# Retention and a gated MLP on one core: moving loads, masks and conversions of the first pairs

## The chip, the cores and the metric

One core of one Trainium2 chip. The time is device microseconds of one execution, over several executions; the traces' span (first to last instruction) is 1.7 to 1.9 us shorter. An execution that is more than 1.5 % above its kernel's fastest is marked slow and left out of ratios. "Pair" is the unit of the first half of the kernel: 128 time steps of two batch rows, all eight heads; there are twelve, and two pairs make a group of 512 tokens for the MLP.

## The reference

A retention layer (linear attention with a decay per head), then an MLP whose gate is h·cos(h):

```python
B, H, S, D = q.shape                       # 4, 8, 768, 64
gamma = 1.0 - 2.0 ** (-5.0 - np.arange(H))
for t in range(S):
    state = gamma * state + k_t^T v_t      # per batch row and head, 64 x 64
    y[:, :, t] = scale * q_t @ state
x = y as (B*S, H*D)                        # 3072 x 512
h = x @ w_in                               # w_in 512 x 2048
out = (h * np.cos(h)) @ w_out              # w_out 2048 x 512, out in fp32
```

Inputs are fp32 in HBM; the kernel works in bf16.

## The kernel before

A pair p passes these stages. q and v are scaled by powers of gamma (`conv_q`, `conv_v`), k is cast (`conv_k`); q and k are transposed by TensorE (`stage_t`) or, from the fifth pair on, by DMA (`stage_t_dma`); `stage_a` makes the scores and `stage_m` masks them on VectorE; `stage_y` makes the output ("Y", copied by ScalarE into `xt`) and updates the state. The MLP's first half is "F" (`unit_f`, or `pair_f` for one pair's 256 tokens; ScalarE makes the cosine, VectorE the product), its second half "O" (`unit_o`). Buffers, with cuts:

```python
PRE = 5                                    # fp32 buffers of q, k, v, two batch rows each
def load(eng, p, names):                   # nc.sync: hardware queue; nc.gpsimd: software queue
    ...
    eng.dma_start(out=t[p % PRE][b], in_=src[...])
def conv_q(p, eng):
    for b in range(2):
        eng.tensor_tensor(out=qs[p % NB][:, b], in0=qf[p % PRE][b], in1=bc(gq, p % NC), op=ALU.mult)
def stage_m(p, item):                      # two masks for one batch row
    ...
        nc.vector.tensor_tensor(out=am[p % 2][b][j], in0=ap[j], in1=mask..., op=ALU.mult)
        banks.give(bk[j])
```

The order in which instructions are written is the order on each engine. The parts that the change touches:

```python
    ...
    load(nc.gpsimd, 3, ("k0", "q0", "k1", "q1", "v0", "v1"))
    load(nc.sync, 4, ("q0", "q1"))                     # fifth pair, at the very start
    load(nc.gpsimd, 4, ("k0", "k1", "v0", "v1"))
    ...
    stage_t(1, True)                                   # one copy on ScalarE, one on VectorE
    attend(1)                                          # scores and masks
    pair_f(0, 0)
    stage_y(1, nc.scalar.copy)
    pair_f(1, 0)
    ...
    for part in range(3):
        for j in range(4):
            unit_o(0, j, part)
            if part == 2 and j == 0:
                stage_t(2, None)
    for b in range(2):
        stage_m(2, stage_a(2, b))                      # third pair: scores, masks
    conv_v(2, nc.vector)                               # then v
    conv_q(3, nc.gpsimd)
    load(nc.sync, 5, ("q0", "q1", "v0"))
    load(nc.gpsimd, 5, ("k0", "k1", "v1"))
    conv_v(3, nc.gpsimd)
    for j in range(4):
        unit_o(0, j, 3)
        if j == 2:
            stage_y(2, nc.scalar.copy)
    ...
    attend(4)
    o_units(1, 0, 4)
    later(4)                                           # Y of the fifth pair, loads of the eighth
    attend(5)
    ahead(6)                                           # seventh pair: conversions
    stage_t_dma(6)
```

Of the kernel before, what the change touches and what calls it, by code (L numbers as in the profile page):

```python
# [30 lines left out]
def kernel(  # L31
# [9 lines left out]
    nc = tc.nc  # L41
# [10 lines left out]
    PRE = 5  # L52
# [11 lines left out]
    def sb(shape, dt, name):  # L64
        return const.tile(shape, dt, name=name)
# [15 lines left out]
    qf = [[sb([128, H, D], FP32, f"qf{i}_{b}") for b in range(2)] for i in range(PRE)]  # L81
    kf = [[sb([128, H, D], FP32, f"kf{i}_{b}") for b in range(2)] for i in range(PRE)]
    vf = [[sb([128, H, D], FP32, f"vf{i}_{b}") for b in range(2)] for i in range(PRE)]
    ob = [sb([128, DM], FP32, f"ob{i}") for i in range(4)]
    NB = 3
    qs = [sb([128, 2, H, D], BF16, f"qs{i}") for i in range(NB)]
    ks = [sb([128, 2, H, D], BF16, f"ks{i}") for i in range(NB)]
    vs = [sb([128, 2, H, D], BF16, f"vs{i}") for i in range(NB)]
# [13 lines left out]

    SRC = {"q": (qf, q), "k": (kf, k), "v": (vf, v)}

    def load(eng, p, names):
        bp, c = divmod(p, NC)
        for n in names:
            t, src = SRC[n[0]]
            b = int(n[1])
            eng.dma_start(  # L110
                out=t[p % PRE][b],
                in_=src[2 * bp + b, :, ds(c * C, C)].rearrange("h t d -> t h d"))

    def load_w_in(r):
# [36 lines left out]
    def bc(g, c):  # L151
        return g[:, c, :].unsqueeze(2).to_broadcast([128, H, D])

    def conv_q(p, eng):
        for b in range(2):
            eng.tensor_tensor(out=qs[p % NB][:, b], in0=qf[p % PRE][b],  # L156
                              in1=bc(gq, p % NC), op=ALU.mult)

    def conv_v(p, eng):
        for b in range(2):  # L160
            eng.tensor_tensor(out=vs[p % NB][:, b], in0=vf[p % PRE][b],  # L161
                              in1=bc(gk, p % NC), op=ALU.mult)

    def conv_k(p, on_act):
        for b in range(2):
            if on_act:
                nc.scalar.copy(out=ks[p % NB][:, b], in_=kf[p % PRE][b])  # L167
            else:
                nc.vector.tensor_copy(out=ks[p % NB][:, b], in_=kf[p % PRE][b])

    def stage_t(p, split, fill=0):
        n = p % NB
        for b in range(2):
            if fill:
                warm(fill * b)
            bank = banks.take()
            tr = bank.bitcast(BF16).rearrange("p (w a t) -> p w a t", w=2, a=HP)
            for w, src in enumerate((qs[n], ks[n])):
                for a in range(HP):
                    nc.tensor.transpose(tr[:, w, a, :], src[:, b, 2 * a : 2 * a + 2, :], ident)  # L180
            if split is None or split and b == 1:
                nc.vector.tensor_copy(out=qkt[n][:, :, b], in_=tr)
            else:
                nc.scalar.copy(out=qkt[n][:, :, b], in_=tr)  # L184
            banks.give(bank)

    def stage_t_dma(p):
        n = p % NB
        for w, src in enumerate((qs[n], ks[n])):
            nc.sync.dma_start_transpose(  # L190
                out=qkt[n][:, w].rearrange("p b a t -> p (b a) t"),
                in_=src.rearrange("p b h d -> p (b h d)"))

    def qt(n, b, a):
        return qkt[n][:, 0, b, a, :]

    def kt(n, b, a):
        return qkt[n][:, 1, b, a, :]

    def stage_a(p, b):  # L200
        n = p % NB
        bk = [banks.take(), banks.take()]
        ap = [t.rearrange("p (a t) -> p a t", a=HP) for t in bk]
        for a in range(HP):
            for j in range(2):
                po = 64 * j
                nc.tensor.matmul(ap[j][:, a, :], lhsT=kt(n, b, a)[po : po + 64, :],  # L207
                                 rhs=qt(n, b, a)[po : po + 64, :],
                                 tile_position=(po, 0))
        return b, bk, ap  # L210

    def stage_m(p, item):
        b, bk, ap = item
        for j in range(2):
            nc.vector.tensor_tensor(  # L215
                out=am[p % 2][b][j], in0=ap[j],
                in1=mask.unsqueeze(1).to_broadcast([128, HP, 128]), op=ALU.mult)
            banks.give(bk[j])

    def stage_y(p, copy_st=nc.vector.tensor_copy):  # L220
        c = p % NC
        n = p % NB
        for b in range(2):
            bank = banks.take()
            yp = bank.rearrange("p (a t) -> p a t", a=HP)
            for a in range(HP):
                if c > 0:
                    for j in range(2):
                        nc.tensor.matmul(  # L229
                            yp[ts(j, 64), a, :], lhsT=stb[p % 2][:, b, a, ts(j, 64)],  # L230
                            rhs=qt(n, b, a), start=True, stop=False,
                            skip_group_check=True)
                for j in range(2):
                    nc.tensor.matmul(  # L234
                        yp[ts(j, 64), a, :], lhsT=vs[n][:, b, 2 * a + j, :],
                        rhs=am[p % 2][b][j][:, a, :], start=(c == 0), stop=True,
                        skip_group_check=True)
            nc.scalar.copy(out=xt[(p // 2) % 2][:, :, ts(2 * (p % 2) + b, C)], in_=yp)  # L238
            banks.give(bank)
        if c == NC - 1:  # L240
            return
        for b in range(2):
            for a in range(HP):
                for j in range(2):
                    h = 2 * a + j
                    nc.tensor.matmul(  # L246
                        st_ps[ts(j, 64), b, a, :], lhsT=ks[n][:, b, h, :],
                        rhs=vs[n][:, b, h, :], start=(c == 0 and b == 0 and a == 0),
                        stop=True, skip_group_check=True)
        for j in range(2):  # L250
            copy_st(out=stb[(p + 1) % 2][ts(j, 64), :, :, ts(j, 64)], in_=st_ps[ts(j, 64)])  # L251
# [21 lines left out]
    def pair_f(p, r, parts=(0, 1)):  # L273

        g, hf = divmod(p, 2)
        for f in [4 * r + 2 * i for i in parts]:
            bank = banks.take()
            for e in range(2):
                for i in range(KIN):
                    nc.tensor.matmul(bank[:, ts(e, 256)], lhsT=w_in_t(i, f + e),  # L280
                                     rhs=xt[g % 2][:, i, ts(hf, 256)],
                                     start=(i == 0 and e == 0), stop=(i == KIN - 1),
                                     skip_group_check=True)
            act(bank, gt[g % 2][:, f : f + 2, ts(hf, 256)])
            banks.give(bank)
# [33 lines left out]
    def attend(p):  # L319
        for it in [stage_a(p, b) for b in range(2)]:  # L320
            stage_m(p, it)
# [8 lines left out]
    load_w_out(3)  # L330
    load(nc.gpsimd, 2, ("v0", "v1"))
    load(nc.gpsimd, 3, ("k0", "q0", "k1", "q1", "v0", "v1"))
    load(nc.sync, 4, ("q0", "q1"))
    load(nc.gpsimd, 4, ("k0", "k1", "v0", "v1"))

    warm(10)
    conv_q(0, nc.vector)
# [7 lines left out]
    warm(6)  # L345
    stage_y(0, nc.scalar.copy)
    warm(2)
    stage_t(1, True)
    attend(1)
    pair_f(0, 0)  # L350
    banks.give(spare)
    stage_y(1, nc.scalar.copy)
    pair_f(1, 0)
    for f in range(4, 16):
        unit_f(0, f)
# [3 lines left out]
    for part in range(3):  # L359
        for j in range(4):  # L360
            unit_o(0, j, part)
            if part == 2 and j == 0:
                stage_t(2, None)
    for b in range(2):
        stage_m(2, stage_a(2, b))
    conv_v(2, nc.vector)
    conv_q(3, nc.gpsimd)
    load(nc.sync, 5, ("q0", "q1", "v0"))
    load(nc.gpsimd, 5, ("k0", "k1", "v1"))
    conv_v(3, nc.gpsimd)  # L370
    for j in range(4):
        unit_o(0, j, 3)
        if j == 2:
            stage_y(2, nc.scalar.copy)
    conv_q(4, nc.gpsimd)
    conv_v(4, nc.gpsimd)
    conv_k(3, True)
    pair_f(2, 0)
    stage_t(3, None)
    pair_f(2, 1)  # L380
    attend(3)
    conv_k(4, True)
    stage_t_dma(4)
    load(nc.sync, 6, ("q0", "q1", "v0"))
    load(nc.gpsimd, 6, ("k0", "k1", "v1"))
    pair_f(2, 2)
    pair_f(2, 3)
    stage_y(3, nc.scalar.copy)
    conv_q(5, nc.gpsimd)
    conv_v(5, nc.gpsimd)  # L390
    pair_f(3, 0)
    conv_k(5, True)
    stage_t_dma(5)
    for r in range(1, 4):
        pair_f(3, r)

    def ahead(p):
        if p < NP:
            conv_q(p, nc.gpsimd)
            conv_k(p, True)  # L400
            conv_v(p, nc.gpsimd)
# [7 lines left out]
    def o_units(g, a, b):  # L409
        for u in range(a, b):  # L410
            unit_o(g, *divmod(u, 4))

    attend(4)
    o_units(1, 0, 4)
    later(4)
    attend(5)
    ahead(6)
    stage_t_dma(6)
    o_units(1, 4, 8)
    later(5)  # L420

    for g in range(2, NG + 1):
        for s in range(16):
            hf, r = divmod(s, 8)
            p = 2 * (g + 1) + hf
# [48 lines left out]
```

## Time and profile before

| | before |
|---|---|
| time, median of 3 executions | 219.04 us (218.5 to 220.6) |
| span of the profiled execution | 217.6 us |
| TensorE / VectorE / ScalarE / GpSimd busy | 94 / 54 / 53 / 39 % |

The page has busy shares, a row per engine of 40 slices in tenths, and TensorE's granted clock in tenths. The chain of waits goes back from the last instruction to what released each step: start, duration in us, engine, tile and line. Of the views behind the prediction one is not shown there, the chain of the kernel before around the seventh pair's scores (L207), from 74 to 104 us:

```profile
79.09 3.47 PE bank L294 x16
82.57 4.65 DMA qkt<-ks
87.21 0.05 issue
87.26 0.62 PE bank L207 x16
```

TensorE's next scores follow a transposing DMA that is issued at 82.57 and lands at 87.21.

### The profile page before, as it was taken

To read this page: it belongs to the slowest core of one execution; us is meant where nothing else is said; L and a number is where in the kernel's file an instruction comes from. 1 tells how busy PE (TensorE), PEld (TensorE's weight loads), DVE (VectorE), ACT (ScalarE), POOL (GpSimd) and SP (SyncE) were. 2 spreads that over 40 slices of the span, in tenths; PEclk is the share of its full clock that TensorE was granted. 3 is DMA by queue.
4 is the path that set the end of the run, shared out by engine and by line. 5 is a ranking of instruction groups with operands and counts; after the bars stand their busy time and mean duration, and the time that the engine had idled before them with its cause. 6 is when DMAs were issued, how large, how long until landed. Compare 5 with 4: busy or idle time off the path is not lost.

```text
span 217.6 us, 4150 instructions
## 1 busy us (share of the span) xinstructions
PE 203.5 (94%) x1637; PEld 114.0 (52%) x1637; DVE 117.2 (54%) x186; ACT 115.0 (53%) x184; POOL 84.9 (39%) x98
## 2 busy tenths in 40 slices
PE   7587999985998998999999999999999999999992
PEld 2357654533898754555554544644545444444440
DVE  4377673465494962786876556656565244333000
ACT  5656873125689545476665565554535644454120
POOL 7975323899996909476951600000000000000000
PEclk9799999998899999999999999999999999999998
DMA  6999999999599889999994551051011001110221
GB/s 150 329 258 196 201 213 289 291 343 344 160 187 275 163 221 197 228 214 259 222 312 102 131 148 48 0 149 48 0 51 48 18 31 51 48 48 2 96 76 71
DMA packets 55844, 33.83 MB, mean 155 GB/s; under 512 B 47248, under 2 KB 49552, under 8 KB 55824
## 3 DMA queue, kind: packets, MB, share of 16 engines
q1 hardware_dynamic: 49472, 17.70, 35.6%
q0 software_dynamic: 6208, 15.73, 27.1%
q8 instruction: 13, 0.21, 0.4%
q10 hardware_dynamic: 144, 0.13, 0.2%
q14 instruction: 7, 0.06, 0.1%
HBM read 27.26 MB, written 6.29 MB: 154 GB/s over the span
## 4 chain that ended last, share of the span: by engine, by line
PE 83%; DVE 6%; DMA 5%; ACT 3%; issue 1%; SPq 0%; DVEq 0%; ACTq 0%
PE bank L294 37%; PE bank L268 30%; PE bank L280 7%; DVE am L215 3%; PE bank L207 3%; DMA qf<-in_q_dram 3%; DMA qkt<-ks 2%; DVE vs L161 2%; PE bank L234 2%; PE bank L229 2%; PE bank L180 1%; PE st_ps L246 1%; ACT xt L238 1%; ACT cosb L259 1%; PE bank L316 1%
## 5 line engine op out<-in xcount | busy, mean ns | idle before, releaser
L263 DVE TENSOR_TENSOR gt<-bank,cosb 128x512 bf16<-128x512 f32 x96 | 65.7, 690 | 63.9 <-ACT cosb L259 63.4
L259 ACT ACTIVATE cosb<-bank,halfpi 128x512 bf16<-128x512 f32 x96 | 65.8, 688 | 54.0 <-PE bank L268 47.5
L294 PE MATMUL bank<-w_out_sb,gt 128*128 128x512 bf16 x384 | 93.9, 382 | 0.0
L268 PE MATMUL bank<-xt,w_in 128*128 128x512 bf16 x304 | 75.0, 380 | 0.0
L294 PEld LDWEIGHTS <-gt 128*128 128x128 bf16 x384 | 36.9, 98 | 43.3 <-issue 0.6
L268 PEld LDWEIGHTS <-w_in 128*128 128x128 bf16 x304 | 33.8, 114 | 30.7
L215 DVE TENSOR_TENSOR am<-bank,mask 128x512 bf16<-128x512 f32 x48 | 30.2, 682 | 4.0 <-PE bank L207 4.0
L306 ACT COPY ob<-bank 128x512 f32<-128x512 f32 x23 | 13.5, 587 | 26.5 <-PE bank L294 26.4
L156 POOL TENSOR_TENSOR qs<-qf,gq 128x512 bf16<-128x512 f32 x18 | 18.6, 1045 | 19.5 <-DMA qf<-in_q_dram 19.3
L161 POOL TENSOR_TENSOR vs<-vf,gk 128x512 bf16<-128x512 f32 x20 | 21.2, 1078 | 5.0 <-DMA vf<-in_v_dram 3.3
L110 POOL DMA_DIRECT2D kf<-in_k_dram x23 | 20.8, 907 | 5.8 <-DMA w_in<-in_moe_w_in_dram 2.8
L280 PE MATMUL bank<-xt,w_in 128*128 128x256 bf16 x160 | 19.0, 277 | 1.3 <-ACT xt L238 1.3
L280 PEld LDWEIGHTS <-w_in 128*128 128x128 bf16 x160 | 17.5, 115 | 2.3 <-issue 1.7
L167 ACT CAST ks<-kf 128x512 bf16<-128x512 f32 x24 | 13.9, 617 | 6.6 <-DMA kf<-in_k_dram 6.5
L110 POOL DMA_DIRECT2D vf<-in_v_dram x16 | 14.2, 889 | 5.0 <-DMA w_out_sb<-in_moe_w_out_dram 4.9
L238 ACT CAST xt<-bank 128x512 bf16<-128x512 f32 x24 | 12.9, 588 | 5.5 <-DVE gt L263 3.0
L234 PE MATMUL bank<-am,vs 128*64 128x128 bf16 x192 | 11.8, 221 | 2.6 <-DVE vs L161 2.2
L234 PEld LDWEIGHTS <-vs 128*64 128x64 bf16 x192 | 10.0, 110 | 3.8 <-DVE vs L161 2.5
L207 PE MATMUL bank<-qkt 64*128 64x128 bf16 x192 | 8.1, 225 | 3.0 <-ACT qkt L184 1.3
L229 PEld LDWEIGHTS <-stb 128*64 128x64 bf16 x160 | 8.7, 109 | 3.8 <-issue 3.3
L229 PE MATMUL bank<-qkt,stb 128*64 128x128 bf16 x160 | 10.6, 223 | 0.0
L251 DVE CAST stb<-st_ps 64x512 bf16<-64x512 f32 x12 | 8.2, 687 | 3.9 <-PE st_ps L246 3.7
(38 smaller groups left out, 73.6 us busy)
## 6 DMA issues: line engine op xcount, KB each, us to landing
kf<-in_k_dram POOLq DMA_DIRECT2D x23, 256.0 KB, 5.9
out_dram<-ob SPq DMA_DIRECT2D x23, 256.0 KB, 2.1
qf<-in_q_dram SPq DMA_DIRECT2D x19, 256.0 KB, 5.0
vf<-in_v_dram POOLq DMA_DIRECT2D x16, 256.0 KB, 6.1
vf<-in_v_dram SPq DMA_DIRECT2D x8, 256.0 KB, 6.5
w_in<-in_moe_w_in_dram POOLq DMA_DIRECT2D x4, 512.0 KB, 13.4
w_out_sb<-in_moe_w_out_dram POOLq DMA_DIRECT2D x4, 512.0 KB, 16.4
qf<-in_q_dram POOLq DMA_DIRECT2D x5, 256.0 KB, 7.6
```

What stands on the lines that cost most here:

```text
L110: eng.dma_start(out=t[p % PRE][b], in_=src[2 * bp + b, :, ds(c * C, C)].rearrange("h t d -> t h d"))
L156: eng.tensor_tensor(out=qs[p % NB][:, b], in0=qf[p % PRE][b], in1=bc(gq, p % NC), op=ALU.mult)
L161: eng.tensor_tensor(out=vs[p % NB][:, b], in0=vf[p % PRE][b], in1=bc(gk, p % NC), op=ALU.mult)
L215: nc.vector.tensor_tensor(out=am[p % 2][b][j], in0=ap[j], in1=mask.unsqueeze(1).to_broadcast([128, HP, 128]), op=ALU.mult)
L229: nc.tensor.matmul(yp[ts(j, 64), a, :], lhsT=stb[p % 2][:, b, a, ts(j, 64)], rhs=qt(n, b, a), start=True, stop=False, skip_group_check=True)
L234: nc.tensor.matmul(yp[ts(j, 64), a, :], lhsT=vs[n][:, b, 2 * a + j, :], rhs=am[p % 2][b][j][:, a, :], start=(c == 0), stop=True, skip_grou ...
L238: nc.scalar.copy(out=xt[(p // 2) % 2][:, :, ts(2 * (p % 2) + b, C)], in_=yp)
L259: nc.scalar.activation(out=cb, in_=bank, func=AF.Sin, bias=halfpi)
L263: nc.vector.tensor_tensor(out=out, in0=bank, in1=cb, op=ALU.mult)
L268: nc.tensor.matmul(bank, lhsT=w_in_t(i, f), rhs=xt[g % 2][:, i, :], start=(i == 0), stop=(i == KIN - 1))
L280: nc.tensor.matmul(bank[:, ts(e, 256)], lhsT=w_in_t(i, f + e), rhs=xt[g % 2][:, i, ts(hf, 256)], start=(i == 0 and e == 0), stop=(i == KIN ...
L294: nc.tensor.matmul(bank, lhsT=gt[g % 2][:, f, ts(j, 128)], rhs=w_out_sb[:, f, :], start=(f == 0), stop=(f == KOUT - 1))
```

## The change

Its intent: keep the hardware DMA queue empty while the weights load (the fifth pair is loaded into the third's buffers, so its loads cannot start before those are read); spread the third pair's scores and masks between O units, with v scaled ahead of the masks; move half an F pair behind the second and the fourth pair's Y; convert and transpose the seventh pair earlier. Cut to its core:

```diff
+    SLOT = [0, 1, 2, 3, 2, 4, 0, 1, 3, 2, 4, 0]        # buffer of each pair, in place of p % PRE
...
-    load(nc.sync, 4, ("q0", "q1"))
-    load(nc.gpsimd, 4, ("k0", "k1", "v0", "v1"))
...
-    stage_t(1, True)
+    stage_t(1, None)                                   # both copies on VectorE
     attend(1)
-    pair_f(0, 0)
+    pair_f(0, 0, (0,))
     stage_y(1, nc.scalar.copy)
+    pair_f(0, 0, (1,))
...
             if part == 2 and j == 0:
                 stage_t(2, None)
-    for b in range(2):
-        stage_m(2, stage_a(2, b))
-    conv_v(2, nc.vector)
+                conv_v(2, nc.vector)
+            elif part == 2 and j == 1:
+                stage_m(2, stage_a(2, 0))
+            elif part == 2 and j == 3:
+                stage_m(2, stage_a(2, 1))
+    conv_k(3, True)
     conv_q(3, nc.gpsimd)
+    load(nc.sync, 4, ("q0", "q1"))
+    load(nc.gpsimd, 4, ("k0", "k1", "v0", "v1"))
+    conv_v(3, nc.gpsimd)
     load(nc.sync, 5, ("q0", "q1", "v0"))
     load(nc.gpsimd, 5, ("k0", "k1", "v1"))
-    conv_v(3, nc.gpsimd)
...
-        if j == 2:
+        if j == 1:
             stage_y(2, nc.scalar.copy)
...
-    pair_f(2, 3)
+    pair_f(2, 3, (0,))
     stage_y(3, nc.scalar.copy)
+    pair_f(2, 3, (1,))
...
+    conv_q(6, nc.gpsimd)                               # ahead of the sixth pair's last F pair
+    conv_k(6, True)
+    conv_v(6, nc.gpsimd)
     pair_f(3, 3)
...
     attend(4)
+    stage_t_dma(6)
     o_units(1, 0, 4)
     later(4)
     attend(5)
-    ahead(6)
-    stage_t_dma(6)
```

Left out of this cut: the old place of `conv_k(3, True)`, and `conv_q(4)` and `conv_v(4)`, which are now written behind `attend(3)`.

More of the change, by code (lines that the diff above doesn't have):

```diff
@@ L110, in load @@
             eng.dma_start(
-                out=t[p % PRE][b],
+                out=t[SLOT[p]][b],
                 in_=src[2 * bp + b, :, ds(c * C, C)].rearrange("h t d -> t h d"))
@@ L155, in conv_q @@
         for b in range(2):
-            eng.tensor_tensor(out=qs[p % NB][:, b], in0=qf[p % PRE][b],
+            eng.tensor_tensor(out=qs[p % NB][:, b], in0=qf[SLOT[p]][b],
                               in1=bc(gq, p % NC), op=ALU.mult)
@@ L160, in conv_v @@
         for b in range(2):
-            eng.tensor_tensor(out=vs[p % NB][:, b], in0=vf[p % PRE][b],
+            eng.tensor_tensor(out=vs[p % NB][:, b], in0=vf[SLOT[p]][b],
                               in1=bc(gk, p % NC), op=ALU.mult)
@@ L166, in conv_k @@
             if on_act:
-                nc.scalar.copy(out=ks[p % NB][:, b], in_=kf[p % PRE][b])
+                nc.scalar.copy(out=ks[p % NB][:, b], in_=kf[SLOT[p]][b])
             else:
-                nc.vector.tensor_copy(out=ks[p % NB][:, b], in_=kf[p % PRE][b])
+                nc.vector.tensor_copy(out=ks[p % NB][:, b], in_=kf[SLOT[p]][b])
     def stage_t(p, split, fill=0):
@@ L363 @@
                 stage_t(2, None)
-    for b in range(2):
-        stage_m(2, stage_a(2, b))
-    conv_v(2, nc.vector)
+                conv_v(2, nc.vector)
[4 more added lines that the diff above has]
+    conv_k(3, True)
     conv_q(3, nc.gpsimd)
+    load(nc.sync, 4, ("q0", "q1"))
+    load(nc.gpsimd, 4, ("k0", "k1", "v0", "v1"))
+    conv_v(3, nc.gpsimd)
     load(nc.sync, 5, ("q0", "q1", "v0"))
     load(nc.gpsimd, 5, ("k0", "k1", "v1"))
-    conv_v(3, nc.gpsimd)
     for j in range(4):
         unit_o(0, j, 3)
-        if j == 2:
+        if j == 1:
             stage_y(2, nc.scalar.copy)
-    conv_q(4, nc.gpsimd)
-    conv_v(4, nc.gpsimd)
-    conv_k(3, True)
     pair_f(2, 0)
@@ L381 @@
     attend(3)
+    conv_q(4, nc.gpsimd)
+    conv_v(4, nc.gpsimd)
     conv_k(4, True)
@@ L393 @@
     stage_t_dma(5)
-    for r in range(1, 4):
-        pair_f(3, r)
+    pair_f(3, 1)
+    pair_f(3, 2)
+    conv_q(6, nc.gpsimd)
+    conv_k(6, True)
+    conv_v(6, nc.gpsimd)
+    pair_f(3, 3)
     def ahead(p):
```

## The prediction

> **What bounds the kernel now.** I read the page first (busy shares, then the slices), then the chain of waits in order of time, TensorE's waits, the timeline where TensorE stopped, and the time to landing of single loads. The page first: row PE is TensorE's busy share of each fortieth of the span (5.44 us), PEclk its granted clock, both in tenths.
>
> ```profile
> PE 203.5 (94%) x1637; PEld 114.0 (52%) x1637; DVE 117.2 (54%) x186; ACT 115.0 (53%) x184; POOL 84.9 (39%) x98
> PE   7587999985998998999999999999999999999992
> PEclk9799999998899999999999999999999999999998
> DMA  6999999999599889999994551051011001110221
> ```
>
> TensorE bounds the kernel; every other engine is near half. Counting slices from 0, there is no hole from slice 16 (87 us) to the last. All that can be won lies before: slices 0 to 3 (to 22 us), slice 9 (49 to 54 us, busy 5, clock 8) with slice 10's clock of 8, and slices 12 and 15. The change touches no matmul: it can only fill holes, and the full stretch after 87 us then starts that much sooner.
>
> The chain of what ended last, 44 to 70 us (start, duration, what):
>
> ```profile
> 44.81 0.37 PE bank L207 x8
> ...
> 45.78 0.55 DVE am L215
> ...
> 46.38 1.28 DVE am L215 x2
> 47.66 4.30 DVE vs L161 x2
> ...
> 53.12 1.82 PE bank L294 x4
> 54.94 2.20 PE bank L280 x16
> ...
> 65.37 0.61 ACT xt L238
> ```
>
> Here the third pair is the trouble: its scores (L207), its four masks on VectorE, then its v scaled on VectorE (L161), then TensorE again. The four O matmuls at 53.12 take 1.82 us where four take 0.86 elsewhere in the same chain, and the 16 of L280 2.20 where 1.74 is usual: half clock, after the stop. At 65.37 TensorE waits for ScalarE's copy of xt. TensorE's waits (us in total, times, longest) give the stops themselves:
>
> ```profile
> PE bank L234 <- DVE vs L161: 2.2, 2, 1.4
> ...
> PE bank L280 <- ACT xt L238: 1.3, 2, 0.8
> PE bank L207 <- DMA qkt<-ks: 0.9, 1, 0.9
> PE bank L207 <- DVE am L215: 0.7, 1, 0.7
> ```
>
> In the timeline (start, duration, engine, line, operation), VectorE's v beside GpSimd's q of the fourth pair:
>
> ```profile
> 46.99 2.05 POOL L156 TENSOR_TENSOR qs<-qf,gq 128x512 bf16<-128x512 f32 x2
> ...
> 47.57 4.37 DVE L161 TENSOR_TENSOR vs<-vf,gk 128x512 bf16<-128x512 f32 x2
> ```
>
> And the hardware queue, where the fifth and sixth pair's loads sit from 6.4 us on (issues on the SyncE sequencer; the first row holds q of both, the second v of the sixth):
>
> ```profile
> 6.36 12.01 SPq L110 DMA_DIRECT2D qf<-in_q_dram  x4
> 18.47 17.00 SPq L110 DMA_DIRECT2D vf<-in_v_dram  x1
> ```
>
> **What the Trainium skill says.** (1) "SBUF — State Buffer", Who interferes with whom: a VectorE instruction with two SBUF inputs contends with a GpSimd instruction that reads SBUF; whoever starts first keeps the shared port. The trace agrees in kind: the two v multiplications (two SBUF inputs) take 4.37 us beside GpSimd, where the same pair takes 2 x 0.69 at 8.06 and 9.57 us; that GpSimd is the cause is argued, not shown. (2) "DMA: Bandwidth & Descriptors", Issuing engines are not separate DMA queues: all queues run on the same 16 engines and interleave. The trace: with the hardware queue loaded, 14 to 28 us moves 199 GB/s, 44 to 52.5 us 338 GB/s; but weights are read as fp32 and counted as bf16, so part of that difference is the counting. (3) "TensorE: Matmul & The Clock Gate", Part 1: the clock halves after about 3.4 us of low activity. The trace has the halved matmuls after 5 us with 2.9 us of stops. (4) "Perfetto Trace Analysis", Identifying the Most-Contended Engine: matmul busy time misleads, since matmuls overlap. Agreed: the L294 row says 382 ns each, but four take 0.86 us in the chain, so I reckon with 0.216.
>
> **The change part by part.**
>
> *Second pair's transposes and the first F pair.* Before, the first copy of the transposed q, k waits on ScalarE behind two state copies (14.79 to 15.96) and runs 15.99 to 17.00; scores start at 17.06, masks 17.49 to 19.97. After, both copies are on VectorE, free at 14.8: first transposes end about 15.2, two copies of 0.69 end about 16.6, masks run 16.65 to 19.13: 0.84 earlier, and Y's end follows the masks. Then L280 started at 21.29 behind the xt copies; now half an F pair (0.87) lies in that wait, so it starts about 19.7 + 0.87 = 20.55. **Gain 0.74.**
>
> *Hardware queue idle.* By 43.84, when the third pair's last v lands, it has moved q of the fifth pair and half of the sixth's q (landed at 18.3, 25.0 and 39.0) and part of the rest: about 0.9 MB of some 11 MB read since 14 us, at 370 GB/s worth 2.4 us; the weights' own landings are spaced 3.3 to 4.4 us while it is busy early and 2.6 later, so perhaps up to 4.8. I take 3: third pair's v at 41, fourth pair's q at 44 instead of 47.15. No weight load stalls TensorE today, so this is worth nothing alone; it makes v come in time to be scaled ahead of the masks.
>
> *Masks between O units, v first.* The O stage starts at 33.39 - 0.74 = 32.65. Nine O units of 0.863: 40.4. Transposes 0.87: 41.3. O unit: 42.15. Scores of half a pair 0.28: 42.4. Two O units: 44.15. Scores: 44.45. Two O units: 46.15. VectorE: copies 41.1 to 42.4, v 42.4 to 43.8 alone; I add 1 us of contention with GpSimd's q (two operations of 1.04 which now start when q lands, 42 to 45): 44.8; masks 44.8 to 47.3. So Y's first half starts at 46.15, its second waits until 47.3: Y and state end at 48.0 (47.5 without contention). Two O units: 49.7. Before, the last O unit ended at 54.94: 5.2 earlier. The 16 of L280 then at full clock save 0.46 more: 5.7, of which 0.74 counted above. **Gain 4.9** (0.7 + 2.2 in listed stops, 1.5 from the clock, the rest masks and start-up of pieces).
>
> *Half an F pair behind the fourth pair's Y.* Removes the 0.8 wait on xt at 66.0, may add 0.2 because the masks have one half pair less to hide behind. **Gain 0.6.**
>
> *Seventh pair's conversions and its transposing DMAs earlier.* The scores at 87.26 wait 0.9 us for qkt by DMA, issued at 80.65 and 82.57. They can now be issued as soon as q and k are converted, some 68 to 72 us, with TensorE there at about 79. **Gain 0.9.**
>
> Sum: 0.74 + 4.9 + 0.6 + 0.9 = 7.1 us; 219.04 - 7.1 = 211.9. No instruction's cost is added; one 1.01 us copy moves from ScalarE to VectorE, which takes 0.69.
>
> **The rivals.**
>
> *GpSimd becomes the pacer.* It is busy 9.87 of the 10 us from 45 to 55 and 10.98 of 11 to 66. It keeps the same work; four issues (0.88 each) of the fifth pair's loads only move behind the fourth pair's q. So it still finishes the fifth pair's conversions near 57.8 and the sixth's near 64.6, as before, while TensorE arrives 6 to 7 us sooner. Sixth pair: its qkt DMAs were issued at 66.0 and 69.9 and landed within 5.8 to 7.4 us; TensorE needs them near 71.5 now (78.5 - 7). Issued from 62.6 with less load traffic beside them, they land at 69 to 72. This is the narrowest place: 0 to 1.5 us lost.
>
> *The late loads collide again.* The fifth pair's q now starts near 35 to 37 and shares the engines with the third and fourth pair's loads; today a load on that queue needed 5.7 to 36.6 us from issue to landing in the stretch from 6 to 18 us. GpSimd wants that q near 53.7, so there are some 17 us; a late one would push GpSimd and the first rival by 1 to 3 us.
>
> *v still slow.* If v lands after 42.4 or GpSimd holds the port throughout (4.37 us again), masks end near 50 and TensorE stops 2.5 us in front of Y, perhaps with the half clock again: gain down to 3 to 4 us.
>
> *A transfer hidden anyway.* True for the weights; the time would then come from the order alone, and I have counted it so.
>
> **Range and chances.** The central sum is 211.9; I allow nothing further for luck and 0.4 for the first rival on average: 212.3. Everything uncontended gives about 210.5 (Y at 47.5, earlier q); two rivals together 215 to 216. Range 209.5 to 216.0. Two per cent is 4.4 us (214.7): only two failures together leave less. Faster 0.85, same 0.14, slower 0.01.
>
> **What would show it.** Right: the v pair of the third pair on VectorE ahead of its four masks at about 42 to 45 us; PEclk without the 8s of slices 9 and 10; last O unit of the first group near 49.7; no wait of L280 on xt over 0.3; no wait for qkt of the seventh pair; the steady part about 7 us earlier, not shorter. Wrong: new waits of the scores for qkt by DMA near 71 us, of GpSimd for q of the fifth pair, of ScalarE for k of the seventh (its copies stand in front of F's cosines), or a v pair still over 4 us.

## The result

| | before | changed |
|---|---|---|
| median, 4 executions each | 219.22 us (218.5 to 220.6) | 212.74 us (211.72 to 213.86) |
| span of the profiled execution | 217.6 us | 210.7 us |
| ratio | | 0.9698, 95 % interval 0.9629 to 0.9767 |

A ratio is the mean time of one kernel's fast runs over that of the other's of the same rounds, so it is not quite the ratio of the medians. Faster by 3.0 % (6.5 us by the medians), 0.4 us from the predicted 212.3.

The changed kernel's page (its lines are numbered two or more higher; its fewer matmuls, x1614, are missing records and not less work, for the weight loads are x1637 as before):

```profile
PE 200.9 (95%) x1614; PEld 113.0 (54%) x1637; DVE 115.0 (55%) x187; ACT 113.6 (54%) x183; POOL 84.3 (40%) x98
PE   7698999999999999999999999999999999999992
PEclk9889999999999999999999999999999999999999
```

The holes of slices 9, 12 and 15 are gone, and so are the two clock dips of 49 to 60 us. Only slices 0 to 3 are left. The chain of the changed kernel, 38 to 72 us (L209 are the scores, L296 O, L282 the F pairs):

```profile
42.65 0.33 PE bank L209 x8
42.97 1.83 PE bank L296 x8
44.81 0.33 PE bank L209 x8
...
48.39 1.67 PE bank L296 x7
50.07 1.75 PE bank L282 x16
...
59.15 7.99 PE bank L282 x72
```

Masks and v are no longer in the chain at all, and 16 matmuls of L282 take 1.75 us at once, full clock. VectorE in the same place (timeline, VectorE alone), with v ahead of the masks and its pair back at 1.28 us from 4.37:

```profile
41.37 1.29 DVE L184 COPY qkt<-bank 128x1024 bf16<-128x1024 bf16 x2 [5.61 <-PE bank L182]
42.58 1.28 DVE L163 TENSOR_TENSOR vs<-vf,gk 128x512 bf16<-128x512 f32 x2
43.78 2.68 DVE L217 TENSOR_TENSOR am<-bank,mask 128x512 bf16<-128x512 f32 x4
```

After the loads of the first two pairs the hardware queue is next used at 35 us (SyncE's timeline, 9 to 85 us); its q loads land 7.4 to 9.2 us after issue, where before they needed up to 36.6:

```profile
35.19 8.35 SPq L112 DMA_DIRECT2D qf<-in_q_dram  x4
```

Where the span went, from the start of each piece on TensorE in the two traces:

| stretch on TensorE | before | changed | won | predicted |
|---|---|---|---|---|
| start to the third pair's transposes | 41.16 | 40.73 | 0.43 | 0.74 |
| to the fourth pair's scores | 18.55 | 13.66 | 4.89 | 4.9 |
| to the fifth pair's scores | 13.39 | 12.68 | 0.71 | 0.6 |
| to the sixth pair's scores | 5.37 | 5.37 | 0 | 0 |
| to the seventh pair's scores | 8.79 | 7.83 | 0.96 | 0.9 |
| to the end | 130.35 | 130.42 | -0.07 | 0 |
| span | 217.61 | 210.69 | 6.92 | 7.1 |

No line is more than 0.31 us off. But a table of two traces does not say which part of the change did what, and the experiments correct that story.

### The profile page after: what moved, and what is told of

It reads as the page before. It is cut to its first block, busy times and chain, and to the rows that moved or that the text cites. A ratio compares the mean times of both kernels' runs of the same rounds, so it can differ in the third digit from the quotient of the medians.

```text
span 210.7 us, 4125 instructions
## 1 busy us (share of the span) xinstructions
PE 200.9 (95%) x1614; PEld 113.0 (54%) x1637; DVE 115.0 (55%) x187; ACT 113.6 (54%) x183; POOL 84.3 (40%) x98
## 4 chain that ended last, share of the span: by engine, by line
PE 90%; DVE 4%; DMA 3%; issue 1%; SPq 0%; ACT 0%; DVEq 0%
PE bank L296 40%; PE bank L270 31%; PE bank L282 8%; PE bank L209 3%; DMA qf<-in_q_dram 3%; PE bank L231 2%; PE bank L236 2%; DVE am L217 2%; PE bank L182 1%; DVE qs L158 1%; PE st_ps L248 1%; PE bank L318 1%; SPq L112 0%; DVE qkt L184 0%; DVE ob L303 0%
## 5 line engine op out<-in xcount | busy, mean ns | idle before, releaser
L296 PE MATMUL bank<-w_out_sb,gt 128*128 128x512 bf16 x372 | 91.8, 379 | 1.1 <-issue 0.5
L270 PE MATMUL bank<-xt,w_in 128*128 128x512 bf16 x294 | 73.7, 380 | 0.4
L296 PEld LDWEIGHTS <-gt 128*128 128x128 bf16 x384 | 36.7, 98 | 42.7
L163 POOL TENSOR_TENSOR vs<-vf,gk 128x512 bf16<-128x512 f32 x20 | 21.0, 1067 | 0.9 <-DMA vf<-in_v_dram 0.8
L282 PE MATMUL bank<-xt,w_in 128*128 128x256 bf16 x160 | 18.6, 273 | 0.0
L282 PEld LDWEIGHTS <-w_in 128*128 128x128 bf16 x160 | 17.1, 114 | 0.5
L236 PE MATMUL bank<-am,vs 128*64 128x128 bf16 x192 | 11.8, 220 | 0.3 <-DVE am L217 0.3
L318 PE MATMUL bank<-gt 128*128 128x512 bf16 x20 | 8.3, 565 | 1.3 <-DVE gt L137 1.3
```

The source lines that it names most:

```text
L163: eng.tensor_tensor(out=vs[p % NB][:, b], in0=vf[SLOT[p]][b], in1=bc(gk, p % NC), op=ALU.mult)
L236: nc.tensor.matmul(yp[ts(j, 64), a, :], lhsT=vs[n][:, b, 2 * a + j, :], rhs=am[p % 2][b][j][:, a, :], start=(c == 0), stop=True, skip_grou ...
L270: nc.tensor.matmul(bank, lhsT=w_in_t(i, f), rhs=xt[g % 2][:, i, :], start=(i == 0), stop=(i == KIN - 1))
L282: nc.tensor.matmul(bank[:, ts(e, 256)], lhsT=w_in_t(i, f + e), rhs=xt[g % 2][:, i, ts(hf, 256)], start=(i == 0 and e == 0), stop=(i == KIN ...
L296: nc.tensor.matmul(bank, lhsT=gt[g % 2][:, f, ts(j, 128)], rhs=w_out_sb[:, f, :], start=(f == 0), stop=(f == KOUT - 1))
```

## The experiments

Ratios are to the kernel before in the same rounds. The changed kernel stands at 0.9698. In the tables of starts, "scores" are TensorE's scores of that pair.

### The hardware queue busy again (e1)

```diff
-    SLOT = [0, 1, 2, 3, 2, 4, 0, 1, 3, 2, 4, 0]
+    SLOT = [p % PRE for p in range(12)]
...
+    load(nc.sync, 4, ("q0", "q1"))                     # at the start again
```

> The changed kernel with one thing undone: the fifth and sixth pair's loads of the hardware queue are issued at the start again (five buffers in turn), all else as changed. Theory: the idle queue lets the weights and the third pair land about 5.5 us sooner (v of the third pair at 38.3 in place of 43.8), and v ahead of the masks needs it. With the queue busy v lands near 43.5, VectorE's v holds the masks up by about 1 to 2 us and the fourth pair's k and q come near 46 to 47: 1.5 to 3 us slower than the changed kernel, 214.5 to 216. Rival: the idle queue is worth nothing because no weight load stalls TensorE; then the time stays within 0.7 us of 212.7.

Measured: 213.38 us median of all four (fast runs 212.66 to 213.65), ratio 0.9708, interval 0.9669 to 0.9747. The theory's 1.5 to 3 us are not there: on top of the rest, the idle queue is worth nothing that these runs can show. One of its four executions, the profiled one, was slow (216.99), so nothing is said from its trace about the edit. It does show what that execution lost: a transposing DMA landed 6.2 us after issue, TensorE stopped 2.4 us for it at the eighth pair's scores, and the granted clock was 0.70 in the next 5.7 us.

### The idle queue alone (e2)

```diff
+    SLOT = [0, 1, 2, 3, 2, 4, 0, 1, 3, 2, 4, 0]        # in the kernel before
-    load(nc.sync, 4, ("q0", "q1"))                     # and both loads of the fifth pair
-    load(nc.gpsimd, 4, ("k0", "k1", "v0", "v1"))       # behind conv_q(3), ahead of conv_v(3)
```

As in the change, `conv_v(3)` thereby comes ahead of the sixth pair's loads, so that "the order of all else as before" is not quite so.

> The kernel before with the idle hardware queue alone (fifth pair in the third's buffers, its loads behind the third pair's v), the order of all else as before. Theory: alone it is worth little, within 1 us of 219.2, since TensorE waits for the masks and for v behind them, not for a load; the third pair's v lands near 38 to 39 and waits some 8 us to be scaled. Rival: sooner loads alone bring most of it (GpSimd's q of the fourth pair is done by 43 and no longer beside VectorE's v): then 3 us or more are won, and VectorE's v pair takes 1.4 us in place of 4.4. A third outcome is that GpSimd's v of the fourth pair takes its place beside VectorE's v, which then still takes over 2.5 us.

Measured: 218.34 us median, ratio 0.9934, interval 0.9861 to 1.0007: 0.7 %, not clear of nothing. The time is what the theory said, the reason is not. On VectorE the v pair, still behind the masks, is down to 1.28 us, because GpSimd's q of the fourth pair was done by 42.8:

```profile
45.22 2.48 DVE L217 TENSOR_TENSOR am<-bank,mask 128x512 bf16<-128x512 f32 x4 [2.07 <-PE bank L209]
47.62 1.28 DVE L163 TENSOR_TENSOR vs<-vf,gk 128x512 bf16<-128x512 f32 x2
```

TensorE reaches the sixth pair's scores at 75.06, 3.4 us ahead of before. Then the chain, 74 to 104 us, a line of TensorE's waits, and a stretch of the windows view (start:end, length, busy time and count of TensorE, its weight loads, VectorE, ScalarE and GpSimd, then granted clock, DMA share, GB/s):

```profile
81.10 4.43 DMA qkt<-ks
85.58 0.62 PE bank L209 x16
86.20 1.22 PE bank L296 x4
87.41 3.17 PE bank L270 x8
```

```profile
PE bank L209 <- DMA qkt<-ks: 2.6, 1, 2.6
```

```profile
85.50:91.00 5.50, 5.42 (x31) 2.36 (x32) 2.35 (x4) 1.07 (x2) 5.02 (x6) 0.69 1.02 232
```

The seventh pair's transposing DMA lands at 85.53; TensorE stops 2.6 us for it, and then runs at half clock for a while: the eight F matmuls take 3.17 us in place of 1.73, and the granted clock from 85.5 to 91 us is 0.69. At the eighth pair's scores both kernels stand at 99.20. In this execution all that was won was given back in one place. It is the slowest of the four (219.31); two others, 216.41 and 217.39, kept part of the gain and have no trace.

### v behind the masks again (e3)

```diff
-                conv_v(2, nc.vector)
             elif part == 2 and j == 1:
                 stage_m(2, stage_a(2, 0))
             elif part == 2 and j == 3:
                 stage_m(2, stage_a(2, 1))
+    conv_v(2, nc.vector)
```

> The changed kernel with VectorE's v of the third pair behind its four masks again, the masks still spread. Theory: v then starts at 46.4, beside GpSimd's v of the fourth pair (46.15 to 48.2), takes 2.5 us or more in place of 1.28, and TensorE stops 1.5 to 3 us in front of Y: 214.5 to 216.5, with a stop on v in TensorE's waits. Rival: the two O units between hide v; then under 0.7 us is lost.

Measured: 212.89 us median of four, one of them slow (215.81), ratio of the fast ones 0.9692, interval 0.966 to 0.9725: the rival in size. In the trace the fourth pair's scores come 0.4 us later. VectorE's v starts at 46.48 as expected, but nothing clashes with it:

```profile
46.48 1.28 DVE L163 TENSOR_TENSOR vs<-vf,gk 128x512 bf16<-128x512 f32 x2
```

GpSimd, in its own timeline, is waiting for that very v (the bracket: 2.31 us, ended by VectorE's L163):

```profile
43.35 1.81 POOL L112 DMA_DIRECT2D kf<-in_k_dram  x2
47.46 1.80 POOL L112 DMA_DIRECT2D vf<-in_v_dram  x2 [2.31 <-DVE vs L163]
```

The fifth pair's v goes into the third's buffer, so GpSimd cannot issue that load before VectorE has read the buffer, and its own v stands behind that load. The shared buffers keep the two engines apart by themselves. I had overlooked it.

### Scores and masks in one piece again (e4)

```diff
-            elif part == 2 and j == 1:
-                stage_m(2, stage_a(2, 0))
-            elif part == 2 and j == 3:
-                stage_m(2, stage_a(2, 1))
+    for b in range(2):
+        stage_m(2, stage_a(2, b))
```

> The changed kernel with the third pair's scores in one piece behind the third part of O, as before, v still ahead of the masks. Theory: the stop of 0.7 us between the halves of the scores returns (the second half waits for a bank that the first mask frees), and the masks end near 47.5 to 47.8, so Y waits another 0.5 us: 0.8 to 1.6 us slower than the changed kernel, about 213.5 to 214.3. Rival: the spreading carries most of the gain; then over 2.5 us are lost.

Measured: 212.98 us median, ratio 0.9695, interval 0.966 to 0.9731: no difference in time, less than both theory and rival said. In TensorE's waits the stop for a bank is back, as expected,

```profile
PE bank L209 <- DVE am L217: 0.7, 1, 0.7
```

and from the third pair's transposes to the fourth's scores it takes 14.39 us in place of 13.66. So spreading is worth 0.7 us in the trace, below what the times resolve.

### The seventh pair late again (e6)

```diff
-    conv_q(6, nc.gpsimd)
-    conv_k(6, True)
-    conv_v(6, nc.gpsimd)
     pair_f(3, 3)
...
     attend(4)
-    stage_t_dma(6)
     ...
     attend(5)
+    ahead(6)
+    stage_t_dma(6)
```

> The changed kernel with the seventh pair's conversions and its transposing DMAs where they were (behind the sixth pair's scores). The working of the prediction gave this part 0.9 us: then about 213.6. New theory, from the run with the idle queue alone (3.4 us ahead at the sixth pair's scores, nothing left at the eighth's): this part is what lets everything won before it stay won. The DMAs then land at 82 to 84 us, TensorE stands at the seventh pair's scores from 80.3, stops for 1.5 to 3.5 us and runs at half clock after it: 2.5 to 5 us slower than the changed kernel, 215.3 to 217.7, PEclk 7 or 8 near 85 to 92 us.

Measured: 216.01 us median of five fast runs (213.64 to 216.83), ratio 0.987, interval 0.9802 to 0.9938: 3.3 us slower than the changed kernel by the medians, 3.8 by the ratios, whose intervals do not overlap. The prediction's step said 0.9. The profiled execution is the fastest of the five. Even there, TensorE's waits have

```profile
PE bank L209 <- DMA qkt<-ks: 1.7, 1, 1.7
```

and from the sixth to the seventh pair's scores it takes 9.61 us in place of 7.83. On SyncE the two transposing DMAs stand behind the three loads of the eighth pair (71.82 to 75.5); they are issued at 75.68 and 77.38 and land at 80.62 and 81.54. GpSimd had converted q by 66.0, ScalarE k by 73.5: q's DMA waited for its place in the queue, not for its data. This execution kept its full clock. The four slower ones lost another 2 to 3 us; a half clock as in e2 would explain it, but they have no trace here, so that is not shown.

### GpSimd's q behind three load issues (e8)

```diff
-    conv_q(3, nc.gpsimd)                               # in the kernel before
     load(nc.sync, 5, ("q0", "q1", "v0"))
     load(nc.gpsimd, 5, ("k0", "k1", "v1"))
+    conv_q(3, nc.gpsimd)
     conv_v(3, nc.gpsimd)
```

> The kernel before with GpSimd's q of the fourth pair moved behind the three issues of the sixth pair's loads, so that GpSimd writes DMA descriptors, not q, beside VectorE's v of the third pair. Theory: the 4.37 us of that v pair come from GpSimd's two reads of SBUF; v then takes 1.3 to 1.6 us, and TensorE is 2 to 4 us ahead at the fourth pair's scores (55.7 to 57.7 in place of 59.7). Rival: issuing loads slows VectorE as well (its second v took 1.53 us beside issues alone); then the pair takes 2.5 us or more. Either way the time stays within 1.5 us of before if the seventh pair's wait takes the gain back.

Measured: the v pair on VectorE and GpSimd's work beside it (timeline of each engine):

```profile
47.45 1.28 DVE L161 TENSOR_TENSOR vs<-vf,gk 128x512 bf16<-128x512 f32 x2
```

```profile
47.01 1.75 POOL L110 DMA_DIRECT2D kf<-in_k_dram  x2
48.75 0.88 POOL L110 DMA_DIRECT2D vf<-in_v_dram  x1
49.65 2.05 POOL L156 TENSOR_TENSOR qs<-qf,gq 128x512 bf16<-128x512 f32 x2
```

1.28 us beside the issuing of loads, 4.37 when it starts beside GpSimd's q. The clash is between the two engines' multiplications, and the rival (issues slow VectorE too) falls for this run. Why the second of the two multiplications still took 1.53 us in the kernel before, when GpSimd was issuing again, stays open (last section). TensorE reaches the fourth pair's scores at 55.83 in place of 59.71. Time: 219.02 us median, but two of four executions were slow (221.39, 225.77); the two fast ones are 216.32 and 216.64, ratio 0.987, interval 0.9784 to 0.9957.

### v ahead of the masks alone (e10)

```diff
                 stage_t(2, None)                       # in the kernel before
+                conv_v(2, nc.vector)
     for b in range(2):
         stage_m(2, stage_a(2, b))
-    conv_v(2, nc.vector)
```

> The kernel before with one line moved: VectorE's v of the third pair ahead of its masks. v lands at 43.8, VectorE is done with it at 44.6, GpSimd's q starts at 47: no clash. Theory: TensorE is 4 us or so ahead at the fourth pair's scores (near 55.5) and at the sixth's (near 74.5), and most of it is lost at the seventh's, which still wait for their DMAs: 217 to 219 in all. Rival (the prediction's sum): its 4.9 us are gained and stay, 214.5.

Measured: fast runs 215.32 and 216.26, ratio 0.9839, interval 0.9749 to 0.993; the other two, the profiled one among them, were slow (219.0 and 219.1). With two fast runs this lies between the theory (217 to 219) and the rival (214.5) and decides nothing: one moved line brought about half of the change in two executions and next to nothing in the other two. The slow trace lists what it lost:

```profile
PE bank L207 <- DMA qkt<-ks: 4.5, 2, 3.3
```

The sixth pair's second transposing DMA, issued at 66.05, landed only at 77.88; TensorE stopped 3.3 us for it and 1.2 us more for the seventh pair's. After the stop of 3.3 us the granted clock was still 1.00. Why that DMA took 11.8 us is not known.

### v ahead and the seventh pair early (e12)

The edit of e10, and in the kernel before the seventh pair's conversions and DMAs moved as in the change.

> The kernel before with two parts of the change: v ahead of the masks, and the seventh pair's conversions and DMAs earlier. Theory: the two together bring most of the change: 4 to 5.5 us, 214 to 215.5, with no long wait for the seventh pair's DMAs. Rival: with the queue busy at the start GpSimd and the DMAs come too late for the earlier seventh pair, and 216.5 or more remain.

Measured: 214.8 us median, all four fast (214.76 to 216.24), ratio 0.981, interval 0.9746 to 0.9873: 4.2 of the 6.6 us. With the hardware queue busy at the start, v came in time:

```profile
42.98 1.46 DVE L161 TENSOR_TENSOR vs<-vf,gk 128x512 bf16<-128x512 f32 x2
44.93 2.48 DVE L215 TENSOR_TENSOR am<-bank,mask 128x512 bf16<-128x512 f32 x4 [0.49 <-PE bank L207]
```

TensorE lists no wait for a transposing DMA. Against the changed kernel's trace, 0.2 us are missing up to the third pair's transposes, 1.1 from there to the fourth pair's scores, 0.9 to the fifth's, and nothing after.

TensorE's starts, traces of fast executions (us from the span's start):

| scores of the | before | e2 | e8 | e6 | e12 | changed |
|---|---|---|---|---|---|---|
| third pair | 44.74 | 44.79 | 44.61 | 42.10 | 44.50 | 42.58 |
| fourth | 59.71 | 56.00 | 55.83 | 53.91 | 55.71 | 54.39 |
| sixth | 78.47 | 75.06 | 74.80 | 71.97 | 74.69 | 72.44 |
| seventh | 87.26 | 85.58 | 84.48 | 81.58 | 82.51 | 80.27 |
| sixth to seventh | 8.79 | 10.52 | 9.68 | 9.61 | 7.82 | 7.83 |
| eighth | 99.20 | 99.20 | 96.42 | 93.53 | 94.53 | 92.29 |

Kernels with the seventh pair late need 8.8 to 10.5 us from the sixth to the seventh pair's scores, and those of them that arrive sooner than before need more (though not in the order of arrival); those with it early need 7.8.

### The second pair as before (e7)

```diff
-    stage_t(1, None)
+    stage_t(1, True)
     attend(1)
-    pair_f(0, 0, (0,))
+    pair_f(0, 0)
     stage_y(1, nc.scalar.copy)
-    pair_f(0, 0, (1,))
```

> The changed kernel with the second pair as before: one of its two transposed copies on ScalarE, the first F pair whole ahead of its Y. The prediction gave this part 0.74 us; the traces so far show O starting 0.4 us sooner in the profiled run, and 0.7 between two runs with early starts. Expected: 0.3 to 0.9 us slower than the changed kernel (213.0 to 213.6), TensorE waiting about 0.5 us for ScalarE's xt at 21 us and about 1 us or more for ScalarE's copy ahead of the second pair's scores. Rival: nothing, as the difference is that of the start from run to run; then equal within 0.2 us.

Measured: 212.68 us median of six, ratio 0.9731, interval 0.969 to 0.9772; the changed kernel's is 212.74 in other rounds. Both expected waits are there,

```profile
PE bank L209 <- ACT qkt L186: 1.1, 1, 1.1
...
PE bank L282 <- ACT xt L240: 0.5, 1, 0.5
```

yet O starts at 33.08 in place of 32.95 (in a trace whose first pair's scores came 0.27 us sooner, at 9.85). The times decide nothing: the medians are equal, the ratios 0.7 us apart, and their intervals overlap.

### The F pair whole ahead of the fourth pair's Y (e5)

```diff
-    pair_f(2, 3, (0,))
+    pair_f(2, 3)
     stage_y(3, nc.scalar.copy)
-    pair_f(2, 3, (1,))
```

> The changed kernel with the half F pair back in front of the fourth pair's Y. The prediction gave this part 0.6 us. Expected: TensorE waits 0.6 to 0.9 us for ScalarE's copies of xt behind that Y; fourth to fifth pair's scores 13.3 to 13.6 us in place of 12.68; 213.3 in all. Rival: the wait is hidden by something else later, equal within 0.2 us.

Measured: 213.26 us median of six, ratio 0.9747, interval 0.9703 to 0.9791. The wait is back,

```profile
PE bank L282 <- ACT xt L240: 0.8, 1, 0.8
```

and from the fourth to the fifth pair's scores it is 13.38 us in place of 12.68, which the span keeps (211.4 in place of 210.7). The times agree in sign (0.5 us by the medians, 1.1 by the ratios), but do not resolve this.

### Two tries to go on (e9, e11)

In the changed kernel a new clash of the same kind appears (VectorE's timeline, then GpSimd's):

```profile
13.23 2.13 DVE L158 TENSOR_TENSOR qs<-qf,gq 128x512 bf16<-128x512 f32 x2
```

```profile
13.34 1.47 POOL L163 TENSOR_TENSOR vs<-vf,gk 128x512 bf16<-128x512 f32 x1 [0.46 <-DMA vf<-in_v_dram]
```

The second pair's v lands sooner (13.27 in place of 14.04), so GpSimd's v falls on VectorE's q, which takes 2.13 us in place of 1.28. The first try moves half of that q ahead of the first pair's masks and one copy to ScalarE:

```diff
+    conv_q(1, nc.vector, (0,))
     attend(0)
     conv_k(1, True)
-    conv_q(1, nc.vector)
+    conv_q(1, nc.vector, (1,))
...
-    stage_t(1, None)
+    stage_t(1, 0)                                      # batch row 0 on VectorE, row 1 on ScalarE
```

> A version that goes on from the changed kernel: in its trace VectorE's q of the second pair takes 2.1 us in place of 1.28, beside GpSimd's v of the second pair, which now comes sooner. Here the first half of that q goes into VectorE's gap ahead of the first pair's masks (its data lands at 9.4 us), and the second of the two copies of transposes goes to ScalarE. Theory: masks of the second pair end 0.4 to 0.7 us sooner and the whole is 0.3 to 0.7 us faster than the changed kernel (212.0 to 212.4). Rival: GpSimd's v still beats the second half of q to the port, or ScalarE's state copies hold its copy up: no gain within 0.2 us.

The second try adds to it, on GpSimd, the first pair's v loads behind the building of identity and mask, and on VectorE the second v between the masks.

> The one before with the first pair's v loaded behind the building of identity and mask on GpSimd, so that the first pair's q and k have the DMA engines to themselves, and VectorE's second v between the masks. Theory: the second q lands at 6.6 to 7.0 in place of 7.46 us, the first scores start up to 0.8 us sooner, 0.3 to 0.8 us faster than the one before it. Rival: the loads of the second pair on the hardware queue fill the room, or v then comes too late for the first Y: no gain, or up to 1 us slower.

Measured: 212.75 us (ratio 0.9719, interval 0.9678 to 0.9761) and 212.42 us (0.9707, interval 0.9668 to 0.9746), six fast runs each. The remaining half of q takes 0.79 us, so the clash is gone; but in the first try ScalarE's copy, behind its state copies, now ends the wait for the scores (0.6 us). In the second, the first pair's last q is scaled at 7.08 us against 7.15 in e5, whose start is that of the changed kernel: the loads did not come sooner. Neither version can be told from the changed kernel, so there is none here that clearly beats it.

## Why the prediction was right, point by point

**The time.** 212.3 predicted, 212.74 measured, inside the range; the stretch-by-stretch sum was 7.1 and came to 6.92 in the two traces, 6.5 by the medians. The 0.4 us between the sum's 211.9 and 212.3 were for GpSimd as the pacer, which did not come: that they brought the number nearer is luck.

**Masks, v and the clock: right.** 4.9 predicted and 4.89 found, including the half clock, which did not come back. That they agree to 0.01 is partly luck: the 1 us of contention allowed for v did not come (1.28 us for the pair), yet Y and the state ended 7.5 us after the transposes began (40.73 to 48.24), where the working has 7.6 with contention and 7.1 without. Of its readings, one is off: the 2.9 us of stops ahead of the half clock lie within 6.8 us (45.2 to 52.0), not 5. That GpSimd's multiplication was the cause of the 4.37 us, which the prediction called argued, is shown by e8. What was wrong is the idea that the parts add: moving the loads (e2), moving GpSimd's q (e8) or moving v (e10, e12) each removes the clash alone, and in the changed kernel two of them are redundant (e1, e3 lose nothing that shows).

**The idle queue: the step failed.** The prediction said "worth nothing alone; it makes v come in time to be scaled ahead of the masks". As to the time, the first half stands (e2: 0.7 %, not clear of nothing), but its reason does not, and the second half is wrong. Alone it puts TensorE 3.4 us ahead at the sixth pair's scores, by letting GpSimd's q finish before VectorE's v starts (e2); and v comes in time without it (42.98 in e12). Its effect on landings was put too low, too: the third pair's last v lands at 38.25 (predicted 41, before 43.84), the fourth pair's last q at 41.44 (predicted 44, before 47.15).

**The seventh pair: right in the table, mis-sized in meaning.** "Gain 0.9" is the stop that the trace before showed, and 0.96 is what the stretch became shorter by. But that stop was sized for a TensorE that arrives late. For one that arrives sooner, the DMAs, queued on SyncE behind the eighth pair's loads, land late by more: 2.6 us of wait and a half clock in the slowest execution of e2, 1.8 of wait in e8, 1.7 in the fastest execution of e6, 3.3 to 3.8 us of time in e6. The step's true worth is that it keeps the others' gain.

**The second pair: mis-sized.** 0.74 predicted; 0.43 in the trace up to the third pair's transposes, of which 0.28 were there at the first pair's scores (10.40 and 10.12), ahead of this edit; undone (e7), the times decide nothing. The new clash on VectorE's q is one reason (TensorE waits 0.4 us for it in the changed kernel).

**The half F pair: right.** 0.6 predicted, 0.7 by the trace of e5.

**The rivals.** GpSimd did not become the pacer in the changed kernel's trace: the sixth pair's DMAs landed at 66.7 and 69.3, TensorE came for them at 72.4. The late loads did not collide: they landed within 9.2 us. (The 5.7 us that the prediction gives as the shortest landing on that queue before is of a load of GpSimd's; the four of the hardware queue needed 12.0 to 36.6.) v was not slow.

**Open.** What the four slower executions of e6 lost beyond the traced one; why single transposing DMAs landed late in the slow executions of e1 and e10, and what slowed those of e8, which have no trace; what ended the two multiplications so late beyond GpSimd's own time (see the last section).

## What to carry to other kernels

Undo each part alone before believing a sum: where several parts remove the same stop, each looks worthless when undone, and where one part guards the others' gain, it looks small in the profile and large when undone. When a change brings an engine forward, go on to the next thing that was just in time, and ask what stands in front of it in its queue; here it was a transposing DMA behind three loads. A buffer shared on purpose can also serve as an interlock between two engines that should not run side by side.

## What the Trainium skill lacked or had wrong

- "SBUF — State Buffer", Who interferes with whom: that VectorE's two-input operation contends with a GpSimd operation that reads SBUF agrees in kind (4.37 us for two beside GpSimd's q, 1.28 beside issues alone in e8). A block until the other's end does not give the size: VectorE started at 47.57, GpSimd's q ended at 49.04, and the two operations, 0.64 each when alone (1.28 for two), ended at 51.94, some 1.6 us later than such a block would have it. The second of them started only at 50.42 and took 1.53. No page says why, and the runs do not either; the spans that this profile gives for GpSimd are rough.
- "TensorE: Matmul & The Clock Gate", Part 1, gives one idle window of about 3.4 us for the half clock. A stop of 2.6 us (e2) was enough for a granted clock of 0.69 in the next 5.5 us, and one of 2.4 us (the slow execution of e1) for 0.70 in the next 5.7; yet a stop of 1.7 us (e6) and one of 3.3 us (the slow execution of e10) left it at 1.00. So the length of the stop alone did not decide it here. In the kernel before, three stops of 0.7, 1.4 and 0.8 us within 7 us gave 0.67 from 52 to 57.2 us.
- "DMA: Bandwidth & Descriptors" gives no time to landing for a load on one queue beside another queue that is full. In the kernel before, a load of 256 KB on the hardware queue needed up to 36.6 us, while from 43 to 52 us the loads of the software queue landed about 0.83 us apart; in the changed kernel, issued from 35 us on, such loads needed 7.4 to 9.2 us.
